# One attention-and-experts kernel, several edits at once: bias MLP in attention buffers, a new issue plan, q/k/v loads behind the scatters, tokens of all experts fetched up front

## The chip, the cores and the metric

The kernel runs on one core of one Trainium2 chip. The metric is device time in microseconds (us), the slowest core of one execution; here there is one core. Runs of one kernel mostly agree within 1% (the kernel before on chip 5: 388.09 to 390.63), but some fall in a slow state, some per cent longer (there 411.82 to 420.15). Chips differ too: the kernel before had fast runs of 382 to 386 on chip 12 and 388 to 391 on chip 5, so each experiment is compared with the kernel before on its own chip.

A ratio in this text is the mean time of one kernel's fast runs over that of the other's fast runs of the same rounds, so it is not quite the ratio of the medians quoted beside it.

Engine names in the profile: PE is TensorE, PEld its weight load, DVE VectorE, ACT ScalarE, POOL GpSimd, SP SyncE. A letter q after a name is that engine's queue.

## The reference, cut to what matters

```python
# q, k, v: 8 sequences x 8 heads x 576 positions x 64
scores = q @ k.T / 8 + bias          # bias: small MLP of log1p(|i-j|) / log1p(max(i,1)), 32 hidden units
attn   = softmax(scores)
x      = (attn @ v) as 4608 rows of 512
# eight experts, one for each row, by domain_id
out[mask_e] = relu(x[mask_e] @ moe_w1[e]) @ moe_w2[e]      # 512 -> 1024 -> 512
```

The bias is the same for all sequences, so the kernel computes its exponential once and multiplies.

## The kernel before

It has four stages: the bias MLP, eight sequences of attention, eight experts, and a tail that no edit touches. A sequence is 21 units. A unit computes a block of scores on PE, takes its exponential on ACT, and then does the jobs that a plan lists for it: T and D are transposes of q and k of the *next* sequence and the copies of their results, V prepares v, W multiplies by the bias on DVE, A is attention times values, N the normalization. A quote mark means that the job belongs to the sequence before.

```python
PLAN = ("A40'", "A41' A42' W0", "A43' N4' V", "", "A30' W2", "A31' A32' W4", "A33' N3'",
        "T0 W6 D0", "A00 A01", "A02 W8", "A03 T4 N0 D4 W9", "T1 D1", ... "T2 D2", "T3 W15 D3", ...)
...
            if b < B - 2 and ui == 3:
                self.load_qk(b + 2)
            if b < B - 2 and ui == 5:
                self.load_v(b + 2)
                self.load_last(b + 2)
            if b < B - 2 and ui == 7:
                self.load_vrag(b + 2)
            late(b, ui)                  # weight loads for the experts, and xA in the last sequence
```

N3' normalizes the last heads of a sequence and issues four scatters of its rows into a token buffer in DRAM, sorted by expert; N4' does the same for the last 64 rows. All loads of q, k, v and weights and all scatters are issued by GpSimd, in one order fixed by the program. xA is a transposing fetch, issued by SyncE, of the first 512 tokens of expert 0; xT are the like for the other tokens. Before, expert e + 2 is fetched while expert e runs.

```python
    xTs = {e: fetch(e) for e in range(2)}
    for e in range(E):
        xT, ids = xTs.pop(e)
        ...                              # first layer
        if e + 2 < E:
            xTs[e + 2] = fetch(e + 2)
        for kk in range(NCH):
            ...
            second(hT, 128 * kk, e, ids[:, kk, :])
            G.w.load(1, G.w_late)
```

The softmax here doesn't subtract the row's maximum and nothing guards it: scores larger than these inputs give would overflow.

## Time and profile before

| | us |
|---|---|
| median of three runs (380.7 to 398.94) | 383.27 |
| time of the profiled run (not one of these three) | 391.34 |
| span of the profiled run | 389.8 |
| bias MLP, up to the first score matmul | 55.7 |
| first sequence | 25.1 |
| second to seventh sequence, each | 19.9 to 20.5 |
| last sequence, up to the first expert matmul | 25.7 |
| experts, up to the end of the last copy of a result | 152.7 |
| tail | 9.2 |

The stages are cut at instants that the timeline shows: the two wide matmuls of unit 0 of each sequence, the first matmul on xA, the last copy from PSUM. The lines themselves stand in the prediction. In a list of stretches, the columns are the stretch, its length, the busy time of PE, PEld, DVE, ACT and POOL with instruction counts, the granted PE clock as a share of full speed, the share of the 16 DMA engines (which can come out over 1), and GB/s. In a timeline, the columns are start, duration, engine and line; the bracket at the end is how long the engine had stood idle, and what ended that. A line of SPq is SyncE's queue: its duration is the time that the queue was busy with a fetch, and the data can land later (in the kernel before, the fetch of xA kept the queue busy for 2.08 us, and PE could start on it 4.9 us after it began).

### The profile page before, as it was taken

Reading aid. Unit: us, or ns where it says so; the run is one execution under the profiler, and the core shown is the slowest. Engines: PE = TensorE matmul, PEld = TensorE weight load, DVE = VectorE, ACT = ScalarE, POOL = GpSimd, SP = SyncE. Lnnn points to the kernel's source line nnn. Section 1 sums busy time; section 2 is a strip of 40 time slices with the busy share of each in tenths; the row PEclk is TensorE's granted clock in tenths of the full one; section 3 lists DMA queues with packets and bytes.
Section 4 is the critical chain, followed back from the end, with each engine's and each line's share of the span. In section 5 each row is a group of like instructions: output and inputs, shape, how many; then the busy total and the mean of one; then the engine's idle time right before and its main releaser. Section 6 shows DMA issues by size and latency. Waiting matters only on the chain. (4 is left out here: it accounts for less than half of the span.)

```text
span 389.8 us, 9399 instructions
## 1 busy us (share of the span) xinstructions
PE 333.9 (86%) x3938; PEld 217.0 (56%) x3938; DVE 238.3 (61%) x456; ACT 249.1 (64%) x303; POOL 173.7 (45%) x220
## 2 busy tenths in 40 slices
PE   1499998699898989899897789999996996999990
PEld 1388764457565656566564545656462554565640
DVE  7999959999899989999999731120302021122120
ACT  8999968789999999999999823315050322332410
POOL 9260006028594958687845242735430055142231
PEclk9999657999999999999999989999999698999996
DMA  5999979909999999999999736999999769021221
GB/s 88 177 163 363 375 268 117 123 0 157 139 142 151 134 150 129 149 131 168 173 214 228 161 88 115 201 203 235 231 228 216 129 98 272 11 109 55 77 82 44
DMA packets 86899, 61.30 MB, mean 157 GB/s; under 512 B 43461, under 2 KB 76997, under 8 KB 86856
## 3 DMA queue, kind: packets, MB, share of 16 engines
q0 software_dynamic: 55808, 45.12, 68.0%
q1 hardware_dynamic: 31048, 15.57, 16.7%
q8 instruction: 31, 0.51, 0.5%
q14 instruction: 12, 0.10, 0.1%
HBM read 61.93 MB, written 24.70 MB: 222 GB/s over the span
## 5 line engine op out<-in xcount | busy, mean ns | idle before, releaser
L556 ACT ACTIVATE e<-sc 128x1024 f16<-128x1024 f32 x168 | 153.0, 1013 | 13.9 <-PE sc L530 10.7
L752 DVE COPY res<-ops 128x512 f32<-128x512 f32 x40 | 27.7, 692 | 123.1 <-PE ops L749 116.6
L805 ACT ACTIVATE hT<-hps 128x640 f16<-128x640 f32 x56 | 39.4, 703 | 90.2 <-PE hps L773 85.3
L567 DVE TENSOR_TENSOR e<-e,biasM 128x2048 f16<-128x2048 f16 x64 | 71.9, 1152 | 1.8 <-ACT e L556 1.5
L773 PE MATMUL hps<-xT,w 128*128 128x320 f16 x448 | 66.7, 312 | 7.2 <-DMA xT<-fire_x 4.2
L749 PE MATMUL ops<-w,hT 128*128 128x512 f16 x320 | 70.5, 379 | 0.0
L753 POOL DMA_INDIRECT out_dram<-res,ids x40 | 39.7, 992 | 60.1 <-DVE res L752 47.1
L773 PEld LDWEIGHTS <-w 128*128 128x128 f16 x448 | 45.5, 102 | 28.6 <-issue 8.0
L530 PE MATMUL sc<-qkT 64*128 64x512 f16 x256 | 49.5, 390 | 9.6 <-ACT e L556 8.3
L749 PEld LDWEIGHTS <-hT 128*128 128x128 f16 x320 | 31.2, 98 | 36.5 <-ACT hT L785 0.3
L641 POOL DMA_INDIRECT fire_x<-xt,posi x32 | 39.0, 1218 | 23.4 <-DMA last<-in_q_dram 8.6
L584 PE MATMUL pu<-vext,e 128*128 128x65 f16 x1024 | 49.4, 195 | 0.0
L584 PEld LDWEIGHTS <-e 128*128 128x128 f16 x1024 | 43.7, 99 | 3.3 <-issue 2.4
L717 POOL DMA_DIRECT2D w<-in_moe_w_dram x32 | 24.7, 781 | 40.5 <-PE hps L773 26.1
L208 DVE TENSOR_SCALAR hr<-L,slope,nb 128x576 f16<-128x576 f16 x116 | 41.5, 438 | 0.0
L225 PE MATMUL eb<-W2BIG,hr 128*128 128x32 f16 x576 | 28.7, 194 | 11.9 <-DVE hr L208 9.0
L580 PE MATMUL pu<-vrag,e 128*128 128x130 f16 x128 | 28.9, 226 | 7.2 <-DVE xt L611 6.0
L225 PEld LDWEIGHTS <-hr 128*128 128x128 f16 x576 | 23.6, 116 | 16.9 <-DVE hr L208 14.4
L641 POOL DMA_INDIRECT fire_x<-xl,posi x8 | 12.4, 1547 | 41.4 <-DVE vext L477 15.7
L530 PEld LDWEIGHTS <-qkT 64*128 64x128 f16 x256 | 14.8, 93 | 25.3 <-issue 15.6
L505 DVE COPY qkT<-pt 128x1024 f16<-128x1024 f16 x32 | 21.9, 685 | 4.3 <-PE pt L480 4.3
L580 PEld LDWEIGHTS <-e 128*128 128x128 f16 x128 | 12.5, 97 | 21.4 <-issue 9.7
(124 smaller groups left out, 373.2 us busy)
## 6 DMA issues: line engine op xcount, KB each, us to landing
w<-in_moe_w_dram POOLq DMA_DIRECT2D x32, 512.0 KB
fire_x<-zero SPq DMA_DIRECT2D x1, 9252.0 KB
qn<-in_q_dram POOLq DMA_DIRECT2D x8, 512.0 KB
kn<-in_k_dram POOLq DMA_DIRECT2D x8, 512.0 KB
vst<-in_v_dram POOLq DMA_DIRECT2D x8, 512.0 KB
out_dram<-res,ids POOLq DMA_INDIRECT x40
last<-zero SPq DMA_DIRECT2D x2, 256.0 KB, 2.6
last<-in_q_dram POOLq DMA_DIRECT2D x16, 32.0 KB
```

What stands on the lines that cost most here:

```text
L208: nc.vector.tensor_scalar(out=hr, in0=G.L4[:, c0: c0 + S], scalar1=G.slope[:, m: m + 1], scalar2=G.nb1[:], op0=AO.mult, op1=AO.max)
L225: nc.tensor.matmul(out=eb[:, lj, 32 * k16: 32 * k16 + 32], lhsT=rap(hr, jc, [[4, 128]]), rhs=G.W2BIG[:, 0:32], start=True, stop=True)
L530: mm(out=sc[:, h2, :], lhsT=self.qkT[b, p][hs[h2], 1, 128 * c: 128 * c + 128], rhs=self.qkT[b, p][hs[h2], 0, :], start=not raw, stop=True)
L556: nc.scalar.activation(out=ef[:, 0:n], in_=sf[:, 0:n], func=AF.Exp, bias=0.0, scale=0.125)
L567: self.nc.vector.tensor_tensor(out=job[0], in0=job[0], in1=job[1], op=AO.mult)
L580: mm(out=self.pu[:, c // 2, o: o + 130], lhsT=er[:, p % 2, 128 * c: 128 * c + 128], rhs=vr[:, p, :], start=True, stop=False, skip_group_ch ...
L584: mm(out=self.pu[:, c // 2, o + 65 * h2: o + 65 * h2 + 65], lhsT=self.e[b, ("m", p, j)][:, h2, 128 * c: 128 * c + 128], rhs=vx[:, 2 * p + ...
L641: inst = self.nc.gpsimd.indirect_dma_start(out=self.x_dram[:, :], out_offset=bass.IndirectOffsetOnAxis(ap=self.G.posi[0:n, c:c + 1], axis= ...
L749: nc.tensor.matmul(out=ops_, lhsT=hT[:, fc, t0: t0 + 128], rhs=G.w.w2(e, fc), start=(fc == 0), stop=(fc == 7))
L753: inst = nc.gpsimd.indirect_dma_start(out=out[:], out_offset=bass.IndirectOffsetOnAxis(ap=idx.bitcast(I32), axis=0), in_=res[:], in_offset ...
L773: nc.tensor.matmul(out=hps[:, i, 0:HC], lhsT=G.w.w1(e, dc)[:, 128 * fc: 128 * fc + 128], rhs=xT[:, dc, HC * hf: HC * hf + HC], start=(dc = ...
L805: nc.scalar.activation(out=hT[:, fc, :].rearrange("p (a b) -> p a b", a=2), in_=first(e, xT, ((fc, 0), (fc, 1))), func=AF.Relu, bias=0.0, ...
```

## The change

Its intent: save SBUF by putting the hidden layer of the bias MLP into buffers that attention uses later, so that expert weights can come early; spread the jobs of a sequence better; and fetch the tokens of all eight experts before the weights crowd them.

```diff
 PLAN = (
-    "A40'",  ...  "T0 W6 D0",  ...
+    "A40' A41' W19'",
+    "V T4",
+    "W0 A42' A43' D4",
+    "T0 N4'",
+    "W2 A30'",
+    "A31' D0 A32' W4",
+    "A33'",
+    "N3' T1",
     [...]
-            if b < B - 2 and ui == 3:
+            if b < B - 2 and ui == 8:
+                self.load_last(b + 2)
                 self.load_qk(b + 2)
-            if b < B - 2 and ui == 5:
+            if b < B - 2 and ui == 10:
                 self.load_v(b + 2)
-                self.load_last(b + 2)
-            if b < B - 2 and ui == 7:
                 self.load_vrag(b + 2)
     [...]  # bias MLP: routing finished before the first sequence; a third tile of odd blocks on ACT
+                for _ in route:
+                    pass
     [...]  # outputs of the last 64 rows in two halves of the partitions, joined by a copy
+            nc.sync.dma_start(out=xl[0:64, 0, 256:DM], in_=xl[64:128, 0, 0:256])
+            self.scatter(b, 4, xl[0:64, 0, :], 64)
     [...]  # last sequence: A4 and N4 at units 19 and 20 instead of after the end
+            return {19: "W16 N2 A40 A41", 20: "A42 A43 W18 N4"}.get(ui, PLAN[ui]).split()
     [...]  # weights (three parts more at the start of attention), and clears of overflow rows by eight scatters
-                    if b < 6 and ui == 10:           G.w.load(1, G.w_first)
-                    if 6 <= b < B and ui == 1:       G.w.load(3, G.w_first)
-                    if 6 <= b < B and ui == 3:       G.w.load(9 - b, G.n4)
+                    if (b, ui) == (0, 2):            G.w.load(2, ...); _clear_overflow(...)
+                    if (b, ui) == (6, 8):            G.w.load(3, ...); G.w.load(2, ...)
+                    if (b, ui) == (7, 11):           G.w.load(2, ...); G.w.load(2, ...)
     [...]
-    xTs = {e: fetch(e) for e in range(2)}
+    xTs = {e: fetch(e) for e in range(E)}
-            G.w.load(1, G.w_late)
+            if e > 0 or kk == NCH - 1:
+                G.w.load(1, G.w_late if 4 < len(G.w.q) < 17 else G.w_first)
```

Some lines of the diff are joined here to save room.

## The prediction

> **What bounds the kernel now.** I read the page first, then busy time by stage, then the timeline of each stage's edges and the queue of the sync engine. No engine bounds the whole span, and the chain that ended last has only two steps, so stages have to be read one by one.
>
> ```profile
> span 389.8 us, 9399 instructions
> ...
> PE 333.9 (86%) x3938; PEld 217.0 (56%) x3938; DVE 238.3 (61%) x456; ACT 249.1 (64%) x303; POOL 173.7 (45%) x220
> ```
>
> Four stages follow from the timeline. Bias MLP: up to the first attention score matmul at 55.7 us. Attention: from there to the first expert matmul at 227.9. Experts: to the last copy of a result at about 380. Tail: some 10 us of last scatter and end of program, which the diff does not touch.
>
> Busy time by stretch (window; PE, PEld, DVE, ACT, POOL in us with counts; PE clock, DMA share, GB/s), first the start of attention, then two ordinary sequences:
>
> ```profile
> 55.70:79.67 23.97, 18.60 (x273) 11.99 (x272) 20.76 (x41) 18.36 (x22) 7.41 (x12) 0.85 0.78 101
> ...
> 118.44:138.97 20.53, 18.66 (x308) 12.82 (x307) 19.46 (x30) 19.03 (x22) 14.53 (x17) 1.00 1.02 146
> 138.97:159.26 20.29, 18.26 (x297) 12.43 (x294) 18.99 (x30) 19.03 (x22) 14.48 (x17) 1.00 0.99 143
> ```
>
> In an ordinary sequence ACT needs 19.03 of some 20.25 us and DVE 19.0: two engines at their limit, with ACT the higher floor. ACT's missing 1.2 us are two holes, both waits for scores:
>
> ```profile
> 114.67 3.13 ACT L556 ACTIVATE e<-sc 128x1024 f16<-128x1024 f32 x4 [0.44 <-PE sc L530]
> ...
> 118.44 3.97 ACT L556 ACTIVATE e<-sc 128x1024 f16<-128x1024 f32 x4 [0.63 <-PE sc L530]
> ```
>
> The first sequence is longer. Its first score matmul is at 55.69 and the second sequence's at 80.75, 25.1 us, against 20.2 on average later. DVE idles just before, then carries 28 small routing operations:
>
> ```profile
> 58.30 0.69 DVE L505 COPY qkT<-pt 128x1024 f16<-128x1024 f16 x1 [4.16 <-PE pt L480]
> ```
>
> Experts, by stretch (each is one expert):
>
> ```profile
> 263.66:280.99 17.33, 17.33 (x106) 10.18 (x105) 3.46 (x5) 5.63 (x8) 9.14 (x11) 1.00 1.18 235
> 280.99:302.70 21.71, 17.49 (x106) 10.12 (x104) 4.15 (x6) 5.63 (x8) 3.95 (x5) 0.98 1.18 222
> 302.70:322.96 20.26, 20.26 (x105) 11.35 (x106) 2.08 (x3) 5.63 (x8) 6.34 (x7) 0.85 0.72 123
> 322.96:345.06 22.10, 19.13 (x105) 10.72 (x104) 4.15 (x6) 5.62 (x8) 7.80 (x9) 0.92 0.44 137
> ```
>
> An undisturbed expert is 17.33 us of gapless PE. Experts 3, 4 and 5 take 4.4, 2.9 and 4.8 us more, 12.1 together. Why, in the timeline:
>
> ```profile
> 266.06 24.07 SPq L762 DMA_TRANSPOSE xT<-fire_x  x1
> 302.70 11.79 PE L773 MATMUL hps<-xT,w 128*128 128x320 f16 x64 [4.22 <-DMA xT<-fire_x]
> 314.79 0.79 POOL L717 DMA_DIRECT2D w<-in_moe_w_dram  x1 [26.12 <-PE hps L773]
> ```
>
> The tokens of expert 4 are asked for only at 266, when weight loads have the DMA engines full (share 1.1 to 1.3 from 240 to 305), and land at 302.7. After that hole PE runs at half clock. Then a weight load with no free buffer holds the GpSimd queue for 26 us, with result scatters behind it; at 323 to 330 the results find no buffer and PE stands again.
>
> [...] after the 4.2 us hole 64 matmuls take 11.79 us, against 8.86 in other experts. [...] Here 16 transposes of 64 columns with alternating halves run in 0.57 us, so about 36 ns each. [...] the same row scatter takes 0.97 us or 2.01 here.
>
> **The change part by part.**
>
> 1. *Bias stage.* The hidden layer goes into attention tiles; reads and writes keep their size. Odd blocks from the third on give 3 tiles to ACT instead of 2: 3 blocks x 0.35 us (13 DVE tiles take 4.52) is 1.0 us off DVE, which sets the pace there; ACT gets 3 x 0.77 more, and it idles 3.0 us at the end of the stage. The clearing of the token buffer falls from 9.25 MB to 5.26 MB, but at 370 GB/s it ran beside other work: no direct gain. Gain 1.0.
>
> 2. *Routing before the first sequence.* The 6 us of small operations fill the 4.2 us hole of DVE and delay its next copy by about 1.5 us. The first sequence should fall from 25.1 to some 20.5 us. Gain 4, taken with the uncertainty of the start.
>
> 3. *New order in a sequence, last-query scores in the transpose buffers.* The holes come where one 256-wide score block (exp 0.40 us) must hide a set of transposes; now the set and that block are apart. Outputs of the last 64 queries in two halves: 40 matmuls at about 36 ns against 20 at about 58 (five in 0.29 us), +0.3 us of PE, which has slack. The normalization of these rows is one operation less, 0.44 us off DVE. ACT floor 19.03 + 0.3: at best 19.4. But the q/k loads now follow four scatters: 4 x 1.28 us (the last four, 229.84 to 233.68, start that far apart), then 2.6 for the last rows, then about 8 from issue to landing of k (108.8 to 116.7 in the trace), 15.7 us in all, and the transposes ask for them 16 units x 0.95 = 15.2 us later. That is even. I put 19.9 instead of 20.24 on six sequences, gain 2, and accept 0 to 5.
>
> 4. *Last sequence.* It has no loads or transposes; the ACT hole there (1 to 1.5 us) shrinks, and its last-query outputs no longer stand between the last exp and the first expert:
>
> ```profile
> 224.89 0.23 PE L580 MATMUL pu<-vrag,e 128*128 128x130 f16 x1 [1.29 <-DVE xl L627]
> ...
> 227.88 8.20 PE L783 MATMUL hps<-xA,w 128*128 128x512 f16 x32 [0.45 <-DMA xA<-fire_x]
> ```
>
> The last exp ends at 223.4, the experts start 4.5 later; some 3 us should do. The early tokens must be there by then: fewer weight loads run before them now, so I expect it. Gain 1 + 1.3.
>
> 5. *Experts.* All eight token fetches go out at once, before the bulk of the weights; 14 weight parts instead of 17 are loaded before the stage, the other 18 go out five per expert with no buffer to wait for. The first expert 18.45 and seven times 17.33 are 139.8, against 152.0 now. Gain 12; I count 11.
>
> Sum: 1.0 + 4 + 2 + 2.3 + 11 = 20.3 us. On the profile 389.8 becomes about 369.5. On the timed median 383.27 becomes 363. The median lies 6.5 under the profiled span; if part of that is smaller expert stalls in the unprofiled runs, part of the gain is already in it. I take back 2: 365.
>
> **The rivals.**
>
> - *Loads become the bound.* If transposes wait for q/k behind the scatters, sequences stay at 20.2 to 20.6, and the second sequence loses more, since eight overflow-clearing scatters (8 x 1.28 = 10 us of GpSimd, from about 59) stand before the loads it needs. For: the even sum in part 3. Against: the DMA engines have room in each sequence (share 0.5 to 0.6 at 120 to 124, where 1.4 and more is reached at 112 to 120)[...]. It would cost 3 to 6 us: 369 to 371.
> - *DMA contention moves rather than goes.* Five weight parts and five result scatters per expert are 3.9 MB in 17.3 us, 226 GB/s, about what 240 to 290 showed with the engines full; the eight fetches come on top. If GpSimd's queue lags by more than the eight result buffers, PE stands[...]. Against: the first expert issues one load only, so the fetches have 18 us nearly alone. It would give back 4 to 8 us: 369 to 373.
> - *ACT becomes the bias bound.* Between the starts of its bias exps ACT takes 4.88 us where it has three tiles (24.87 to 29.75) and 4.12 where it has two; a DVE block of 13 takes 4.63. It would turn gain 1 into 0.
> - *All holes close and sequences reach 19.4*: another 3 us, 360 or less.
>
> **Range and chances.** The expert gain rests on stalls that are seen with their causes, the attention gain on a schedule. Both rivals together still leave about 373; the best case is near 357. The three timed runs of before scatter by 18 us, so the upper end gets room. Faster by over 2% means under 375.6: 0.91. Within 2%: 0.08. Slower: 0.01.
>
> **What would show it.** Right: each expert at 17.3 us, no PE wait for xT, no half clock after the start of the experts; the first two score starts some 20.5 us apart; later ones 19.4 to 20.2; the expert stage starting at about 218.6. Wrong: PE waiting at the transposes for qn or kn, GpSimd waiting long before scatters into the output, result copies waiting for their DMA, or xA later than the last attention matmul by over 1 us.

## The result, and the profile after

The changed kernel is slower. Its median is 410.26 us of four runs (408.06 to 442.76, the longest slow), against 391.11 for the kernel before in the same rounds (four runs, 380.7 to 406.43). The ratio of the fast runs is 1.0749, with a 95% interval of 1.0636 to 1.0862. The profiled run of the kernel before took 391.34 us, 8 to 11 us more than its two fast timed runs (383.27 and 380.7), while that of the changed kernel (408.06) is like its others. So the profiles below show a loss of 16.7 us where the fast runs lost some 28. Where the other 11 lie was not profiled; the part on the prediction comes back to it.

The page of the changed kernel begins so:

```profile
span 406.5 us, 9749 instructions
...
PE 334.1 (82%) x4098; PEld 215.8 (53%) x4098; DVE 235.1 (58%) x450; ACT 250.9 (62%) x306; POOL 186.6 (46%) x228
```

The busy times of PE, DVE and ACT differ from before by 0.2, 3.2 and 1.8 us. So the 16.7 us more of span are not work but waiting. A table by stage says where they lie:

| stage | before | after | difference |
|---|---|---|---|
| bias MLP | 55.69 | 55.57 | -0.1 |
| first sequence | 25.06 | 24.14 | -0.9 |
| second sequence | 20.36 | 19.59 | -0.8 |
| third to seventh sequence, together | 101.10 | 122.42 | +21.3 |
| last sequence, up to the first expert matmul | 25.67 | 34.13 | +8.5 |
| experts | 152.73 | 141.62 | -11.1 |
| tail | 9.19 | 9.03 | -0.2 |
| span | 389.8 | 406.5 | +16.7 |

The experts did what was hoped. Two things went wrong, both in attention. First the ordinary sequences. These are stretches of the changed kernel: the first sequence, the second, and the fourth, fifth and seventh:

```profile
55.57:79.71 24.14, 20.44 (x276) 12.78 (x275) 21.98 (x44) 19.34 (x24) 15.53 (x19) 0.79 0.39 46
79.71:99.30 19.59, 18.33 (x319) 12.22 (x318) 18.64 (x29) 18.88 (x22) 9.78 (x10) 1.00 0.63 96
...
125.54:149.81 24.27, 20.23 (x319) 13.20 (x319) 18.78 (x29) 19.17 (x22) 14.38 (x18) 0.86 0.71 100
149.81:174.06 24.25, 20.02 (x319) 13.14 (x318) 18.78 (x29) 19.11 (x22) 14.47 (x18) 0.86 0.73 101
...
197.41:221.72 24.31, 20.05 (x318) 13.06 (x318) 18.85 (x29) 19.11 (x22) 13.24 (x18) 0.86 0.74 109
```

The busy columns of ACT and DVE stay near 19, as before, while the length is 24.3: both engines now stand still for about 5 us in each sequence, and PE runs at a lower mean clock (0.86, against 1.00 in the second sequence). What they wait for is in the timeline of the fourth sequence, just after its start:

```profile
130.35 0.58 PE L534 MATMUL pt<-idn,qn 128*64 128x128 f16 x8 [1.64 <-DMA qn<-in_q_dram]
132.99 0.64 PE L534 MATMUL pt<-idn,kn 128*64 128x128 f16 x8 [2.05 <-DMA kn<-in_k_dram]
...
134.21 1.02 ACT L613 ACTIVATE e<-sc 128x1024 f16<-128x1024 f32 x1 [4.12 <-PE sc L587]
```

The transposes of unit 3 find q not landed, then k. The next scores come after them in PE's program, and ACT has nothing for 4.12 us. And why the loads are late is on GpSimd's queue of the same sequence:

```profile
138.88 1.74 POOL L698 DMA_INDIRECT fire_x<-xt,posi  x1 [1.56 <-DVE xt L670]
140.92 1.39 POOL L698 DMA_INDIRECT fire_x<-xt,posi  x1 [0.30 <-issue]
142.61 1.18 POOL L698 DMA_INDIRECT fire_x<-xt,posi  x1 [0.30 <-issue]
144.10 1.43 POOL L698 DMA_INDIRECT fire_x<-xt,posi  x1 [0.30 <-DMA fire_x<-xt,posi]
145.53 1.34 POOL L512 DMA_DIRECT2D last<-in_q_dram  x2
146.82 1.28 POOL L512 DMA_DIRECT2D last<-in_k_dram  x2
148.02 0.99 POOL L504 DMA_DIRECT2D qn<-in_q_dram  x1
148.91 0.98 POOL L504 DMA_DIRECT2D kn<-in_k_dram  x1
```

And the end of PE's wait for this k, in the fifth sequence:

```profile
157.48 0.64 PE L534 MATMUL pt<-idn,kn 128*64 128x128 f16 x8 [2.59 <-DMA kn<-in_k_dram]
```

Four scatters, then the last rows, then q and k. The k of this list ended PE's wait at 157.48, 18.6 us after the first of these scatters began. The scatters begin only when unit 7 has been normalized, and unit 7 comes after the transposes of unit 3. So the path closes on itself: late transposes make late scatters, which make late loads, which make late transposes. From k landed (132.99) to the first scatter (138.88) it takes 5.9 us and on to the next k 18.6 us, together 24.5 us. That is the length of a sequence.

The second loss is the last sequence. Weight loads, xA, and the first expert matmul of the changed kernel:

```profile
239.51 3.01 POOL L781 DMA_DIRECT2D w<-in_moe_w_dram  x4
241.30 10.16 SPq L983 DMA_TRANSPOSE xA<-fire_x  x1
...
255.85 3.57 PE L847 MATMUL hps<-xA,w 128*128 128x512 f16 x8 [10.33 <-DMA xA<-fire_x]
```

Four weight parts of 512 KB are issued just before the fetch, which is as large as one of them (512 tokens of 512 values of 2 bytes). The queue is busy with it for 10.16 us, PE can start 14.55 us after the fetch began (before, it landed 4.9 us after its issue), and PE stands for 10.33.

The experts, by contrast, run without a hole. Two stretches of one expert each; before, the like lines were 20.26 to 22.10 us long:

```profile
290.60:307.93 17.33, 17.33 (x106) 10.14 (x104) 3.46 (x5) 5.63 (x8) 9.02 (x11) 1.00 1.21 226
307.93:325.26 17.33, 17.33 (x106) 10.15 (x104) 3.46 (x5) 5.63 (x8) 8.94 (x11) 1.00 1.22 234
```

### The profile page after: what moved, and what is told of

Its sections match the earlier page's. It is cut to its first block, busy times and chain, and to the rows that moved or that the text cites. A ratio compares the mean times of both kernels' runs of the same rounds, so it can differ in the third digit from the quotient of the medians.

```text
span 406.5 us, 9749 instructions
## 1 busy us (share of the span) xinstructions
PE 334.1 (82%) x4098; PEld 215.8 (53%) x4098; DVE 235.1 (58%) x450; ACT 250.9 (62%) x306; POOL 186.6 (46%) x228
## 5 line engine op out<-in xcount | busy, mean ns | idle before, releaser
L817 POOL DMA_INDIRECT out_dram<-res,ids x40 | 39.5, 987 | 78.4 <-DVE res L816 65.5
L813 PE MATMUL ops<-w,hT 128*128 128x512 f16 x320 | 70.5, 379 | 0.0
L837 PE MATMUL hps<-xT,w 128*128 128x320 f16 x448 | 62.0, 299 | 0.0
L698 POOL DMA_INDIRECT fire_x<-xt,posi x32 | 43.0, 1343 | 33.1 <-DMA xl<-xl 13.8
L587 PE MATMUL sc<-qkT 64*128 64x512 f16 x256 | 54.1, 417 | 4.8 <-ACT e L613 3.6
L837 PEld LDWEIGHTS <-w 128*128 128x128 f16 x448 | 43.7, 98 | 18.2
L641 PE MATMUL pu<-vext,e 128*128 128x65 f16 x1024 | 53.0, 202 | 0.3 <-DVE e L624 0.3
L641 PEld LDWEIGHTS <-e 128*128 128x128 f16 x1024 | 47.0, 103 | 2.2 <-issue 0.8
L698 POOL DMA_INDIRECT fire_x<-xl,posi x8 | 10.7, 1338 | 55.6 <-DMA xl<-xl 45.6
L240 PE MATMUL eb<-W2BIG,e 128*128 128x32 f16 x432 | 19.9, 193 | 16.0 <-DVE e L223 10.7
L559 DVE COPY qkT<-pt 128x1024 f16<-128x1024 f16 x32 | 21.9, 684 | 16.8 <-PE pt L534 16.7
L223 DVE TENSOR_SCALAR e<-L,slope,nb 128x576 f16<-128x576 f16 x86 | 31.2, 433 | 0.0
L240 PEld LDWEIGHTS <-e 128*128 128x128 f16 x432 | 17.7, 117 | 18.2 <-DVE e L223 11.2
L534 PE MATMUL pt<-idn,kn 128*64 128x128 f16 x256 | 15.0, 246 | 13.6 <-DMA kn<-in_k_dram 13.6
```

The source lines that it names most:

```text
L223: nc.vector.tensor_scalar(out=hr, in0=G.L4[:, c0: c0 + S], scalar1=G.slope[:, m: m + 1], scalar2=G.nb1[:], op0=AO.mult, op1=AO.max)
L240: nc.tensor.matmul(out=eb[:, lj, 32 * k16: 32 * k16 + 32], lhsT=hr[:, jc: jc + 4 * 127 + 1: 4], rhs=G.W2BIG[:, 0:32], start=True, stop=True)
L587: mm(out=sc[:, h2, :], lhsT=self.qkT[b, p][hs[h2], 1, 128 * c: 128 * c + 128], rhs=self.qkT[b, p][hs[h2], 0, :], start=not raw, stop=True)
L641: mm(out=self.pu[:, c // 2, o + 65 * h2: o + 65 * h2 + 65], lhsT=self.e[b, ("m", p, j)][:, h2, 128 * c: 128 * c + 128], rhs=vx[:, 2 * p + ...
L698: inst = self.nc.gpsimd.indirect_dma_start(out=self.x_dram[:, :], out_offset=bass.IndirectOffsetOnAxis(ap=self.G.posi[0:n, c:c + 1], axis= ...
L813: nc.tensor.matmul(out=ops_, lhsT=hT[:, fc, t0: t0 + 128], rhs=G.w.w2(e, fc), start=(fc == 0), stop=(fc == 7))
```

## The experiments

Theory A: the loads behind the scatters are the bound of the third to seventh sequence, and the four weight loads before xA cost the last one its 10 us; the rest of the change is sound. Rivals: the new plan itself costs the time (the early transposes, or the copy of the last rows), or the half clock does. Twelve runs were made in four jobs, each on another chip (chip 12, 5, 1 and 6 below); the fast runs of before had a mean of 384.8, 389.2, 384.9 and 383.4 there.

### 1. The loads at units 3, 5 and 7, as before (chip 12)

```diff
-            if b < B - 2 and ui == 8:
-                self.load_last(b + 2)
-                self.load_qk(b + 2)
-            if b < B - 2 and ui == 10:
-                self.load_v(b + 2)
-                self.load_vrag(b + 2)
+            if b < B - 2 and ui == 3:
+                self.load_qk(b + 2)
+            if b < B - 2 and ui == 5:
+                self.load_v(b + 2)
+                self.load_last(b + 2)
+            if b < B - 2 and ui == 7:
+                self.load_vrag(b + 2)
```

> The changed kernel with one edit: q/k loads at unit 3, v and last rows at 5, ragged v at 7, as in the kernel before (in front of the scatters). Theory A (transposes three units into a sequence wait for q and k that were issued behind four scatters; loop of about 24.3 us): sequences 2 to 6 fall from 24.3 to 19.4 to 20.2 us, PE waits no more for qn or kn, the profile falls by about 20 us to some 386. Rival B (the new order itself, with early transposes, half-column matmuls and the copy of the last rows, makes a sequence long): sequences stay above 23 us and the time stays above 400. The wait for xA before the experts (10.3 us) stays in both.

Median 385.55 (384.54 to 425.35), ratio to before 0.9979 (0.9893 to 1.0065). Second and fourth sequence, and then the fetch of xA and the first expert matmul:

```profile
80.20:104.58 24.38, 20.08 (x319) 13.20 (x319) 18.88 (x29) 19.30 (x22) 11.85 (x13) 0.86 1.02 119
...
123.38:142.28 18.90, 18.26 (x318) 12.24 (x318) 18.61 (x29) 18.84 (x22) 14.16 (x17) 1.00 0.96 137
```

```profile
219.00 9.41 SPq L984 DMA_TRANSPOSE xA<-fire_x  x1
...
232.82 3.57 PE L848 MATMUL hps<-xA,w 128*128 128x512 f16 x8 [10.12 <-DMA xA<-fire_x]
```

Moving three blocks of loads brings the third to seventh sequence to 18.8 to 18.9 us, with ACT busy for all but 0.1 of it; experiment 3, which leaves the loads behind the scatters, has 23.4 to 26.9 us for them in the same job. The span is 23 us below that of the change, whose profile is from another job. The half clock goes with the waits: the granted clock of the fourth sequence is 1.00, against 0.86. That settles the first half of theory A: plan and early transposes are sound, and their sequences shorter than before's, once their data is there. Two losses stay. xA still waits 10 us. And the second sequence takes 24.4: the loads for the third stand behind the eight clears of overflow rows, which GpSimd issues from 61.2 to 71.9, and PE waited 4.04 us for the last rows (which stand behind q, k and v here; the change issues them first, and has no such wait in its second sequence).

### 2. The transposes late as before, the loads behind the scatters as in the change (chip 12)

```diff
-    "V T4",
+    "V",
-    "W0 A42' A43' D4",
+    "W0 A42' A43'",
-    "T0 N4'",
+    "N4'",
     [...]  # T0 to unit 7, D0 and T4 to 8 and 10, T1 to 11, T2 to 15, T3 to 16
```

> The changed kernel with the loads left behind the scatters, but the transposes back at the units of the kernel before (first set at 7, last rows at 10, then 11, 15, 16). If only the deadline counts (theory A), q and k get 4 units or some 3.8 us more, about what PE waits for them now (3.6 to 4 us a sequence): sequences of 20 to 21 us, time about 390. If the place of the loads itself does harm (they collide with something else), sequences stay above 22.5 us.

Median 394.38 (394.0 to 394.85), ratio 1.0223 (1.0155 to 1.029). Sequences of 20.4, 20.9, 24.0, 20.4, 20.4 and 21.9 us. Waits for k fall from 13.6 us (six times) to 4.2 (three times). So four units more between load and use open most of the loop, from the other end. But this plan needs 20.4 us even in the sequences where k comes in time, so against before nothing is won, and the time is 4 us above the 390 that was expected.

### 3. The four weight loads behind the early half of the first expert (chip 12)

```diff
-                    if (b, ui) == (7, 11):
-                        G.w.load(2, G.n4)
-                        G.w.load(2, G.w_first)
     [...]
                 first_early(hT, G.early, fc)
+            G.w.load(2, G.n4)
+            G.w.load(2, G.w_first)
```

> The changed kernel with the four weight loads of unit 11 of the last sequence moved behind the first expert's early half. Theory C (these four loads starve the transposing fetch of the early tokens xA): xA lands some 5 us after its issue instead of 14.5, PE waits 0 to 3 us instead of 10.3, time some 8 to 9 us less, about 401. Rival (xA is late because the scatters before it are late): xA is issued no earlier, and if its landing still takes over 10 us the time stays at 408 to 410.

Median 409.07 (405.1 to 410.5), ratio 1.058 (1.0485 to 1.0676). xA keeps SyncE's queue busy for only 2.08 us now and its wait is gone, but the time hardly moves, where the theory had 401. The fetch of xA, and the timeline a little later:

```profile
241.75 2.08 SPq L982 DMA_TRANSPOSE xA<-fire_x  x1
...
253.70 3.03 POOL L781 DMA_DIRECT2D w<-in_moe_w_dram  x4
255.29 2.22 SPq L826 DMA_TRANSPOSE xT<-fire_x  x1
...
266.04 3.60 PE L855 MATMUL hps<-xT,w 128*128 128x128 f16 x32 [7.93 <-DMA xT<-fire_x]
```

The same four loads now stand in front of the fetch of the rest of expert 0's tokens, and PE waits 7.93 us there. The wait has been handed to the next fetch.

### 4. Experiments 1 and 3 together (chip 12)

> Loads early and the four weight loads behind xA together. Theory A and C: the two gains add, 20 + 9 us, so about 379 to 381 in the profile, below the kernel before (about 390) because the experts keep their 11 us. If they do not add, over 385.

Median 385.44 (384.18 to 386.6), ratio 0.9983 (0.9912 to 1.0054): no better than experiment 1 alone. The reason is that of experiment 3, with 8.82 us of wait:

```profile
243.10 3.60 PE L856 MATMUL hps<-xT,w 128*128 128x128 f16 x32 [8.82 <-DMA xT<-fire_x]
```

### 5. The last rows and the odd bias blocks as before (chip 5, one run)

Outputs and normalization of the last 64 rows as before, without the copy between partitions, and two tiles instead of three on ACT in odd blocks of the bias MLP:

```diff
-                if k16 in ((2, 5, 8, 11, 14) if ib < 2 else (3, 8, 13)):
+                if k16 in ((2, 5, 8, 11, 14) if ib < 2 else (3, 8, 13) if ib % 2 == 0 else (5, 11)):
     [...]
-            nc.sync.dma_start(out=xl[0:64, 0, 256:DM], in_=xl[64:128, 0, 0:256])
-            self.scatter(b, 4, xl[0:64, 0, :], 64)
+            self.scatter(b, 4, xl[:, 0, :], 64)
```

> The changed kernel with two of its parts undone: the outputs of the last 64 queries as before (whole columns, normalization straight into 64 partitions, no copy from one half of the partitions to the other), and in the bias stage two tiles on ACT in odd blocks as before. Theory A (the loads behind the scatters are the bound; the bias stage is bound by ACT): sequences 2 to 6 stay at 24 to 25 us and the bias stage still ends within 0.7 us of 55.6, if anything earlier; the time falls at most 4 us, and only because the scatter of the last rows of the seventh sequence no longer waits some 10 us for its copy, so that xA can start earlier: 405 to 410 on a kernel before of 385 to 390. Rival B (the copy of the last rows, 5 us, sits in the loop of every sequence): sequences fall by 3 us or more, 390 or less.

406.85 us in one run, where before had fast runs of 388.1 to 390.6. The third to seventh sequence take 22.8 to 25.1. Rival B falls: the copy is not what makes the loop long. The fetch of xA starts 3.6 us earlier in its sequence, as the theory hoped, but still lands 16.4 us after its issue, with the same four weight loads in front of it. The bias stage ended at 56.08; in experiment 7, of the same job, which keeps the third tile on ACT, it ended at 55.52. So the third tile is worth about 0.6 us, by one profile each.

### 6. Early loads, and the four weight loads at the end of the first expert (chip 5)

```diff
+            if (e, kk) == (0, NCH - 1):
+                G.w.load(2, G.n4)
+                G.w.load(2, G.w_first)
             if e > 0 or kk == NCH - 1:
```

> The changed kernel with the q/k/v loads at units 3, 5 and 7 as before, and the four weight loads of the last sequence put off to the end of the first expert (after its fifth result). Theory: in the runs before, these four loads starved whichever token fetch stood nearest behind them (10 us of wait for xA, or 8 to 9 us for the rest of expert 0's tokens). With no weight load in front of either, both fetches take about 2 to 4 us, no matmul of expert 0 waits over 1.5 us for tokens, and about 10 us go against the kernel with early loads alone: ratio to before 0.97 to 0.975, 373 to 376 where before shows 385. Rival: the eight fetches starve each other, or the weights for experts 2 and 3 now come late: a wait for xT or for a weight tile over 3 us stays, and the time stays at 380 to 385.

Median 394.56 (390.95 to 410.32), ratio 1.0087 (1.0004 to 1.017). The theory missed by 4%. The profiled run was slow, so its times are not compared; the next kernel has the same edit and a fast profile.

### 7. The same, with the clears behind the loads of the first sequence (chip 5)

```diff
                     if (b, ui) == (0, 2):
                         G.w.load(2, G.w_first)
+                    if (b, ui) == (0, 8):
                         _clear_overflow(tc, G, x_dram)
```

> As the kernel with early loads and late weights, and the eight clears of the overflow rows moved from unit 2 of the first sequence to unit 8, behind the loads for the third sequence. Theory: the second sequence takes 24.4 us there only because these loads stand behind the clears on GpSimd's queue; it falls to 19 us and the time by another 5 us: ratio 0.955 to 0.962, 368 to 371 where before shows 385. Rival: the first sequence lies in the way by itself (PE at half clock, copies of DVE), or the clears now hold up the rows of the first sequence: under 2 us gained.

Median 400.47 of four runs; the two fast ones are 391.7 and 396.47, so their mean is 1.0125 of before's 389.2. A second miss. Two causes can be seen. The first is in the experts. Fetches of tokens on SyncE's queue, and what PE waited for:

```profile
248.85 6.89 SPq L827 DMA_TRANSPOSE xT<-fire_x  x1
...
256.46 27.76 SPq L827 DMA_TRANSPOSE xT<-fire_x  x1
...
285.02 26.02 SPq L827 DMA_TRANSPOSE xT<-fire_x  x1
```

```profile
323.64 11.58 PE L838 MATMUL hps<-xT,w 128*128 128x320 f16 x64 [5.66 <-DMA xT<-fire_x]
349.43 10.65 PE L838 MATMUL hps<-xT,w 128*128 128x320 f16 x64 [5.58 <-DMA xT<-fire_x]
```

Only 10 weight parts are there before the experts (14 in the change, 17 in the kernel before), and five are issued at once at 250.0, so from the end of expert 0 on loads follow one another, 21 of them from 250.0 to 325.34. Only the four fetches issued before that are quick (1.2 to 6.9 us). The others take 12 to 28 us each on the queue, one after the other, and two come late, each followed by a slower matmul group (11.58 and 10.65 us, against 8.86).

The second cause is in attention. No transpose waited over 1 us for data in the second sequence any more, as intended. Yet it took 24.0 us, because at its end (and at the end of the first) PE, ACT and DVE all stood for 2.6 to 2.9 us, and the trace names no instruction that released them: it says `remote` for ACT and DVE and `issue` for PE, which goes on with the first wide score matmul of the next sequence. The slow profile of experiment 6 has three such stalls at the same place; no other profile has one, neither those of experiments 5 and 8 on this chip nor that of experiment 10, which has the clears at the same unit. What they are stays open.

### 8. The kernel before with the new experts alone (chip 5, and again on chip 6)

The part of the change that concerns fetches and weights in the experts; 16 parts are loaded before the stage.

```diff
-    xTs = {e: fetch(e) for e in range(2)}
+    xTs = {e: fetch(e) for e in range(E)}
     [...]  # eight buffers for xT and ids instead of three; 11 and 12 for the weights instead of 12 and 14
-        if e + 2 < E:
-            xTs[e + 2] = fetch(e + 2)
-            G.w.load(1, G.w_late)
+            if e > 0 or kk == NCH - 1:
+                G.w.load(1, G.w_late if 4 < len(G.w.q) < 17 else G.w_first)
     [...]
                     if 6 <= b < B and ui == 1:
-                        G.w.load(3, G.w_first)
+                        G.w.load(9 - b, G.w_first)
```

> The kernel before with the expert part of the change alone: all eight token fetches up front, eight buffers for them, 16 weight parts before the stage, weight loads in the experts from the end of the first on, into buffers that are free. Theory: the gain of 11 us that the prediction counted for this part is there by itself: experts without stalls, 140 to 142 us instead of 152, ratio 0.970 to 0.976, 374 to 376 where before shows 385. Rival: before's attention still issues weight loads close to the token fetches, so a wait for tokens of 4 us or more stays, or the unprofiled runs of before had no such stalls and the gain is half of that.

Median 377.95 (377.75 to 378.41), ratio 0.9718 (0.9661 to 0.9774), inside what was expected. The fetches:

```profile
249.24 5.67 SPq L762 DMA_TRANSPOSE xT<-fire_x  x1
255.58 3.13 SPq L762 DMA_TRANSPOSE xT<-fire_x  x1
259.39 17.09 SPq L762 DMA_TRANSPOSE xT<-fire_x  x1
```

Seven of the nine fetches are done with on the queue before the weights crowd them; the last two take 17 and 26 us there and hold nobody up. No matmul on xA or xT waits for one. All experts run at 17.33.

### 9. Early loads, and weights moved forward (chip 1)

16 parts before the stage as in experiment 8, but none in the last sequence.

```diff
-                    if (b, ui) == (7, 11):
-                        G.w.load(2, G.n4)
-                        G.w.load(2, G.w_first)
+                    if (b, ui) in ((1, 10), (3, 10)):
+                        G.w.load(1, G.w_first)
+                    if (b, ui) == (5, 10):
+                        G.w.load(2, G.w_first)
+                    if (b, ui) == (6, 18):
+                        G.w.load(2, G.n4)
```

> The changed kernel with the q/k/v loads at units 3, 5 and 7 as before, and the weights moved forward instead of back: two parts more than in the change (one each in the second and fourth sequence), two in the sixth and two at the end of the seventh, none in the last sequence, so that 16 parts are there before the experts and 16 remain, as in the kernel before with the new experts. Theory: with no weight load near xA, nor near the token fetches of the first 18 us of the experts, neither the 10 us wait for xA nor the two waits of 5.6 us for late tokens (which came when nine weight parts were asked for at the end of expert 0) appear; most sequences 18.9, the second 24 (clears in front of its loads), experts 140: ratio 0.965 to 0.978. Rival: any place of the weights starves something, and one wait for tokens or rows over 5 us stays: 0.985 or more.

Median 381.57 of four runs, two of them slow; the fast ones are 376.82 and 374.37, ratio 0.9759 (0.9592 to 0.9926). As expected, with a wide interval. The profiled run was slow.

### 10. The same, with the clears behind the loads (chip 1, and again on chip 6)

The edits of experiments 1, 7 and 9 together, 7 with its clears alone.

> The same with the eight clears of the overflow rows at unit 8 of the first sequence, behind the loads for the third sequence. Theory: no transpose of the second sequence waits for its last rows; the second sequence takes 19 to 20 us instead of 24 to 25: another 4 to 5 us, ratio 0.953 to 0.967, and the best of all kernels here. Rival: the stall of some 2.8 us with no visible cause that stood at the end of the first and second sequence in the last runs comes again whatever stands on GpSimd's queue: then the gain is under 2 us.

Three of its four runs on chip 1 were slow, as were five of before's seven there. The one fast run is 370.91, where before's are 383.99 and 385.75. So it was run again, beside the kernel of experiment 8:

> The last kernel once more (early loads, weights moved forward, clears behind the loads), as only one of its four runs fell in the fast state. Theory: 0.955 to 0.970 of the kernel before with a real interval, and below the kernel before with the new experts alone by 0.5 to 1.5%: its sequences take 18.9 us instead of 20.3, seven times, of which some 4 us are lost again where xA is waited for. Rival: the stalls of the slow runs belong to this kernel and not to the chip: half of its runs again over 390, and no gain over the new experts alone.

> The kernel before with the new experts alone, once more, beside the one above on the same chip: 0.970 to 0.976 as before. If both are equal within their intervals, all that the change does outside the experts is worth nothing even when its loads are put right.

This kernel: median 373.6 of six runs, all fast (372.47 to 376.14), ratio 0.9745 (0.9678 to 0.9812). Before with the new experts alone: median 375.73 (374.57 to 376.74 in the fast state), ratio 0.9789 (0.9719 to 0.9858). The fast runs of the one, mean 373.8, lie 0.5% under those of the other, mean 375.5. So both expectations of a size were a little too hopeful. The order is as expected, but the two intervals overlap, and by the test that the second expectation set itself, a gain from the rest of the change is then not shown. Slow runs are no trait of this kernel: on chip 6 none of its runs was slow, and seven of before's twelve were. First to fourth sequence of this kernel:

```profile
55.47:79.64 24.17, 20.49 (x277) 12.82 (x276) 21.93 (x44) 19.35 (x24) 10.98 (x14) 0.79 0.80 101
79.64:98.48 18.84, 18.36 (x318) 12.31 (x318) 18.66 (x29) 18.78 (x22) 14.02 (x17) 1.00 0.85 104
98.48:117.32 18.84, 18.26 (x318) 12.40 (x318) 18.58 (x29) 18.80 (x22) 12.02 (x16) 1.00 0.88 139
117.32:140.13 22.81, 20.77 (x318) 13.70 (x318) 19.06 (x29) 19.42 (x22) 15.36 (x20) 0.85 0.96 132
```

The second sequence is 18.84: with the clears behind the loads its 5 us are gone. The fourth shows what my own edit cost. Two lines of GpSimd's queue in the third sequence, and one of PE in the fourth:

```profile
104.38 0.77 POOL L782 DMA_DIRECT2D w<-in_moe_w_dram  x1
...
109.34 1.27 POOL L512 DMA_DIRECT2D last<-in_q_dram  x2
```

```profile
120.54 1.01 PE L534 MATMUL ptl<-idn,last 128*128 128x128 f16 x8 [1.78 <-DMA last<-in_q_dram]
```

The weight part that I put at unit 10 of the second sequence is issued after the scatters and right before the loads for the fifth; the last rows come 1.78 us late, PE goes to half clock (a mean of 0.52 from 120 to 125), and the sequence takes 4 us more than its neighbours. That this load is the cause is read from the trace, not tested, and it can't be the whole of it: the (slow) profile of experiment 9 has the same part at the same unit with the clears early, and waits there for 0.66 us, with a sequence of 19.35.

In the same job the ordinary sequences of the kernel before (with new experts) took 19.4 to 19.6 us, against 18.85 here, so the new plan with its data in time is worth some 0.75 us for each, by one profile each. On chip 5 the third to seventh sequence took 20.5 on average with the old plan (experiment 8) and 19.55 with the new one (experiment 7).

## Why the prediction was wrong

Predicted were 365 us (356.5 to 374) and 0.91 for faster; measured were 410.26, 7.5% slower than before. By its parts:

1. *Bias stage, gain 1.0.* Measured 0.1 for the stage, by the two profiles; experiment 5 puts the third tile alone at 0.6. The rival "ACT becomes the bias bound" came true in part: after, PE waits 4.0 us for ACT's evictions in this stage, a wait that before does not show among its larger ones.

2. *Routing before the first sequence, gain 4.* Measured 0.9. "delay its next copy by about 1.5 us" is the step that failed: routing runs as one block on DVE from 53.95 to 60.68, and the copy behind it starts at 60.59 instead of 58.30. Two lines of the changed kernel:

```profile
61.33 0.41 PE L534 MATMUL pt<-idn,qn 128*64 128x128 f16 x8 [2.00 <-DVE qkT L559]
...
62.38 1.02 ACT L613 ACTIVATE e<-sc 128x1024 f16<-128x1024 f32 x1 [1.99 <-PE sc L587]
```

   The transposes wait for that copy, ACT for the scores behind them, and PE stays near 0.66 of its clock from 55.5 to 70.5, where before it was back at 0.91 from 65.5. The first half of the sequence takes 13.75 us instead of 10.5; the second half takes 10.4 instead of 14.6, which is the gain that I saw coming. I counted one side.

3. *New order in a sequence, gain 2.* This is the step that decided. I wrote "15.7 us in all, and the transposes ask for them 16 units x 0.95 = 15.2 us later. That is even." Measured from the first scatter to k are 18.6 us: scatters 6.65 instead of 5.1 (1.66 each; the 1.28 was read off the last four, at the end of attention), last rows 2.5, issue of q before k 0.9, which I left out, and k landing 8.6 after its issue instead of 8. The lack of some 3.4 us is about the 3.9 us that PE waited for q and k. The larger mistake is what I made of "even". I took it as a draw, with "accept 0 to 5" of gain, and sized the rival "Loads become the bound" at 3 to 6 us in all, with sequences of 20.2 to 20.6. But the transposes come before the scatters in the next turn, so every sequence pays again: five times 4.3 us. The rival was the right story, at the wrong size and the wrong chance. Experiment 1 shows it: the same plan with early loads has sequences of 18.85 us, below the 19.4 that I had called the best (ACT was busy for 18.8, not for 19.03 + 0.3).

4. *Last sequence, gain 2.3.* Measured a loss of 8.5. "fewer weight loads run before them now, so I expect it" looked at the count of loads and not at their place. The four that are left are issued 1.8 us before xA. Experiments 3 and 4 show that the cost hangs on the place; in experiment 10, which has no weight load there, the wait for xA is 1.07 us. The prediction's own sign of being wrong, "xA later than the last attention matmul by over 1 us", came true with 10.33.

5. *Experts, gain 11 counted.* Between the two profiles 11.1, and each expert after the first took the 17.33 us that was forecast: the mechanism was right. Experiment 8 has the gain by itself, on two chips: 0.9718 is 11.0 of 389.2 us, 0.9789 is 8.1 of 383.4. But 11.1 can't simply be taken for the gain in time. The doubt "if part of that is smaller expert stalls in the unprofiled runs" was measured with unlike things, a span (389.8) and a time (383.27): the profiled run took 391.34, so the gap was 8 us, of which 2 were taken back. In the table the stages of attention alone lose 28.1 us, and some 28 is what the fast runs lost. On chip 12, too, the profile of experiment 1 is 6.4 us shorter than before's, while its fast runs are equal to before's. Both would fit if before's timed runs there had smaller stalls in the experts; no profile of such a run was kept, so this stays open.

The sum had no term for a wait that closes on itself, and its range came from adding gains. A computation that comes out even says that the wait is about as likely as not; 0.01 for "slower" left no room for it.

Of the best version's gain in experiment 10, some four fifths come from the experts alone (2.1 of 2.6 per cent). The half per cent that is left for the rest of the change, with its loads put right, is within the intervals.

## What to carry to other kernels

When a load is moved behind a store, follow the path once around: if the data of the load releases, in the next turn, the work that the store waits for, the turn can't be shorter than this path (24.5 us here), and a lack of a few microseconds (here some 3.4) is paid in every turn. Count bulk loads by where they stand in the queue, not only by how many they are: a fetch on which the next stage waits should have none just in front of it (four of them went with a wait of 10.33 us here), and moving the bulk load by a few units can merely hand the wait to the next fetch (7.93 us in experiment 3). And where the parts of a change don't need each other, test each by itself: here the experts' part brought most of the gain to be had, and the places of the loads hid it.

## What the traces show of the clock and of a fetch behind loads

- The granted clock fell to half around one gap of 1.64 us, which ended with eight transposes at 130.35. In these stretches of the changed kernel the clock, the third number from the end, falls from 1.00 to 0.50; the mean of 0.73 in the middle one puts the fall at about 130.46 (an estimate, if it fell in one step), less than 2 us after the last scores and before the second gap, of 2.05 us, began. It stays there until 137, 4 us after PE is busy again.

```profile
129.00:130.00 1.00, 0.00 (x0) 0.00 (x0) 0.94 (x2) 1.00 (x2) 0.00 (x0) 1.00 1.27 159
130.00:131.00 1.00, 0.58 (x8) 0.34 (x8) 0.61 (x1) 0.10 (x1) 0.00 (x0) 0.73 1.42 193
131.00:132.00 1.00, 0.00 (x0) 0.00 (x0) 0.00 (x0) 0.00 (x0) 0.00 (x0) 0.50 1.44 195
```

- The transposing fetch of xA, of 512 KB, kept SyncE's queue busy for 2.08 us with no weight load just before it (experiment 3), and for 10.16 with four loads of 512 KB issued 1.8 us before it (the changed kernel). Two fetches of 640 KB, with such loads following one another, took 27.76 and 26.02 there (experiment 7).
